# Value blocks placed from PSUM by masked evictions, spread vectors by column strips, and a new order, in a transformer block with sliding attention and a token mixer

## The chip, the cores and the metric

The kernel runs on one core of one Trainium2 chip. The metric is the device time of one execution in microseconds (us); lower is better. The engines are TensorE (PE in the profile, its weight loads PEld), VectorE (DVE), ScalarE (ACT), GpSimd (POOL) and SyncE (SP), whose queue issues almost all DMAs.

## The reference

x is 2048 tokens of 512 features, in bf16. A modulation vector of six parts scales and shifts two branches: sliding-window attention, then a two-layer MLP that mixes along the tokens.

```python
mod = (silu(c) @ w_mod).reshape(1, 6, 1, 512)          # sa, ca, ga, sb, cb, gb
h = layernorm(x) * (1 + ca) + sa
q, k, v = split(h @ wqkv)                              # 32 heads of 16
scores = q @ k.T * 16 ** -0.5, kept where 0 <= i - j < 256
x = x + ga * (softmax(scores) @ v) @ wo
h = layernorm(layernorm(x) * (1 + cb) + sb)
u = gelu(einsum("bsd,sf->bdf", h, w1) + b1)            # over the 2048 tokens, F = 1792
x = x + gb * (einsum("bdf,fs->bds", u, w2) + b2).T
```

## The kernel before

The tokens are cut into four groups of 512 (G = 0 to 3). `proj(G)` normalizes a group, turns it over by DMA (h1T) and multiplies it with wqkv; `attention(G)` runs its scores, exps, masks and sums; `post(G)` multiplies with wo, adds the residual (x) and normalizes twice (h, hb). The first layer of the MLP sums over tokens, so parts of it (pu, part) are done as soon as a group's hb stands, between the chunks of attention; what is left runs after the last group, and then the second layer (py), 238 matmuls in a row, with a store per 128 tokens.

**Keys and values for tiled matmuls.** Scores use rows of 32 and AV sums use column strips of 32, so heads of 16 lie in pairs. Keys (kb, then KT) and values (vb, then VT) are stored twice over, each copy with half of the heads set to zero by a mask per partition (`mask_par`, `mask_half`). A value block `pv` of 128 tokens comes out of PSUM in one cast to `vb` (operation "ve", VectorE or ScalarE); then `place` writes its two halves into VT, `vo` and `vp`, on GpSimd or VectorE. There are four such blocks per group, numbered tb = 0 to 3. Group 0 has its own path, with both halves in one operation.

**Spread vectors.** ga, 1 + cb, sb and gb are needed on all 128 partitions, as rows of 512 (`bc_ga`, `bc_cb1`, `bc_sb`, `bc_gb`). For each, four matmuls with the modulation's silu(c), repeated over 128 columns (`sT_rep`), give the same row on every partition (`ps_b`), and VectorE evicts it. `wod` is wo scaled by bc_ga; the first `post` needs it (`pa`). The others come into `h` (bc_cb1, bc_sb) and into the MLP (bc_gb).

**PSUM.** Scores have five banks (`pss`, three wide, and two of `psb`); all other matmuls share three banks (`ps_od`, tags od0 to od2): projections, AV sums (`po`), wo, the parts and the spread vectors. An operation that takes such a bank waits until what its earlier user put there is evicted.

**Order.** Each operation is an `op` with its possible engines. Two tables set what happens: ORDER, a list of 1,136 numbers, in which the operations are emitted one after the other, and CHOSEN, which takes an operation off its first engine. `run_schedule` emits them so, each engine's instructions keep that order, and every engine and SP's queue run their own list in turn, waiting by semaphores. It also sets `tiled` for runs of projections between AV sums: such a full matmul is then written as four column strips (`mm`), which spares TensorE a change of tiling. All engine calls go through one wrapper, so almost every row of the profile carries its line, L254; rows are told apart by the names of their tiles.

## Time and profile before

| | us |
|---|---|
| runs | 256.61, 259.86, 258.86 (median 258.86) |
| profiled execution | 257.62 |
| its span, first to last instruction | 255.8 |
| busy: TensorE, VectorE, ScalarE, GpSimd | 240.1, 205.5, 172.8, 134.2 |
| last AV sum ends, rest of MLP layer 1 ends | about 178, about 205 |

The span is shorter than the time by 1.8 us of launch and end. A busy time is a union over the span, so it says little of a stage: ScalarE is nearly idle after 181 us, and GpSimd has nothing at all there, while both are close to full between 12 and 120 us.

### The profile page before, as it was taken

How to read it: one execution, taken by the hardware profiler on the slowest of the kernel's cores; microseconds unless marked ns; L12 is line 12 of the kernel's file. 1: busy time of each engine (PE TensorE's matmuls, PEld its weight loads, DVE VectorE, ACT ScalarE, POOL GpSimd, SP SyncE). 2: the span in 40 equal slices, each digit the busy share in tenths (PEclk: the TensorE clock that was granted, in tenths of full speed). 3: DMA queues.
4: the chain of work that ended last, by engine and by line, in shares of the span. 5: the costliest groups of instructions: out<-in, count | busy, mean ns of one | idle time of the engine just before them, and what ended most of it. 6: DMA issues, size and time to landing. Idle time of an engine off the chain costs nothing.

```text
span 255.8 us, 11463 instructions
## 1 busy us (share of the span) xinstructions
PE 240.1 (94%) x5125; PEld 137.7 (54%) x5125; DVE 205.5 (80%) x378; ACT 172.8 (68%) x288; POOL 134.2 (52%) x220
## 2 busy tenths in 40 slices
PE   7999988999889889997999898999999999999995
PEld 3666655656656555655566455557444444444443
DVE  5599998999989979989798879898977974444443
ACT  4699998999998999997899898988207620000000
POOL 6069938967597599969787679964000000000000
PEclk9999999999999999999999999999999999999999
DMA  6998340381032100000621913401699901111111
GB/s 200 327 351 279 68 26 3 82 128 49 3 67 44 27 3 5 4 6 3 177 77 46 249 44 85 122 8 45 179 347 393 352 24 44 41 41 42 60 44 41
DMA packets 39657, 26.44 MB, mean 103 GB/s; under 512 B 11960, under 2 KB 35512, under 8 KB 39608
## 3 DMA queue, kind: packets, MB, share of 16 engines
q1 hardware_dynamic: 39600, 25.71, 35.4%
q8 instruction: 40, 0.66, 1.1%
q14 instruction: 9, 0.07, 0.1%
q10 hardware_dynamic: 8, 0.00, 0.0%
HBM read 22.03 MB, written 2.10 MB: 94 GB/s over the span
## 4 chain that ended last, share of the span: by engine, by line
PE 68%; DVE 16%; ACT 7%; issue 3%; DMA 2%; SPq 2%; POOL 1%; ACTq 0%
PE py L254 19%; PE pu L254 18%; PE po L254 8%; PE pss L254 7%; ACT et L254 7%; DVE et L254 5%; PE pa L254 4%; PE pk L254 3%; PE pq L254 3%; PE pv L254 3%; DVE h L254 2%; DMA x<-in_A_x_dram 2%; DVE st L254 2%; SPq L254 2%; DVE kb L254 2%
## 5 line engine op out<-in xcount | busy, mean ns | idle before, releaser
L254 ACT ACTIVATE et<-pss 128x1536 bf16<-128x1536 f32 (+2 forms) x90 | 101.5, 1147 | 12.0 <-PE psb L254 8.0
L254 PE MATMUL py<-guT,w2r 128*128 128x512 bf16 (+2 forms) x238 | 48.5, 366 | 0.0
L254 ACT ACTIVATE et<-psb 128x512 bf16<-128x512 f32 (+2 forms) x90 | 43.6, 508 | 0.0
L254 DVE TENSOR_TENSOR et<-et,maskt 128x2048 bf16<-128x2048 bf16 (+2 forms) x38 | 42.1, 1120 | 0.4 <-ACT et L254 0.4
L254 PEld LDWEIGHTS <-KT 32*128 32x128 bf16 (+1 forms) x1856 | 24.4, 97 | 30.4 <-issue 26.0
L254 PE MATMUL pu<-hb,w1s 128*32 128x512 bf16 (+1 forms) x260 | 38.8, 380 | 0.8 <-DVE part L254 0.7
L254 PE MATMUL pss<-QT,KT 32*64 32x32 bf16 (+7 forms) x1392 | 34.8, 202 | 4.8 <-ACT et L254 2.2
L254 PE MATMUL po<-et,VT 128*32 128x256 bf16 (+2 forms) x960 | 33.4, 234 | 3.8 <-DVE vb L254 2.2
L254 PEld LDWEIGHTS <-w2r 128*128 128x128 bf16 x238 | 22.8, 98 | 25.9
L254 PE MATMUL psb<-QT,KT 32*128 32x224 bf16 (+3 forms) x464 | 34.3, 203 | 0.9 <-issue 0.9
L254 PE MATMUL po<-et,ones_bd 128*32 128x256 bf16 (+3 forms) x624 | 31.4, 269 | 0.5 <-issue 0.5
L254 DVE TENSOR_TENSOR otile<-py,xr 128x512 bf16<-128x512 f32 (+2 forms) x17 | 11.2, 660 | 24.6 <-PE py L254 24.5
L254 POOL TENSOR_SCALAR KT<-kb,mask_par 128x512 bf16<-128x512 bf16 (+1 forms) x30 | 21.1, 714 | 13.2 <-DVE kb L254 11.8
L254 PEld LDWEIGHTS <-VT 128*32 128x32 bf16 x960 | 21.7, 96 | 10.8 <-issue 3.8
L254 DVE BATCH_NORM_STATS2 st<-x 128x6 f32<-128x512 bf16 x32 | 21.3, 680 | 2.0 <-DMA x<-in_A_x_dram 1.9
L254 POOL TENSOR_SCALAR VT<-vb,mask_half 128x512 bf16<-128x512 bf16 x25 | 20.1, 810 | 4.9 <-DVE vb L254 4.4
L254 PEld LDWEIGHTS <-w1s 128*32 128x32 bf16 (+1 forms) x260 | 13.9, 97 | 14.5 <-issue 1.2
L254 PE MATMUL pk<-h1T,wqkv 128*32 128x512 bf16 (+4 forms) x222 | 20.7, 333 | 0.0
L254 PEld LDWEIGHTS <-wqkv 128*32 128x32 bf16 (+1 forms) x380 | 15.2, 96 | 8.8 <-issue 1.1
L254 PE MATMUL pu<-hb,w1r 128*128 128x512 bf16 (+1 forms) x84 | 18.0, 380 | 0.0
L254 PE MATMUL pv<-wqkv,h1T 128*32 128x256 bf16 x512 | 17.6, 274 | 0.1
L254 PE MATMUL pa<-wod,OT 128*32 128x512 bf16 (+1 forms) x130 | 16.7, 381 | 0.2 <-DVE x L254 0.2
(107 smaller groups left out, 365.3 us busy)
## 6 DMA issues: line engine op xcount, KB each, us to landing
w2r<-in_B_w_dram SPq DMA_DIRECT2D x14, 512.0 KB, 10.5
w1s<-in_B_w_dram SPq DMA_DIRECT2D x19, 256.0 KB, 3.3
w1r<-in_B_w_dram SPq DMA_DIRECT2D x9, 256.0 KB, 4.9
x<-in_A_x_dram SPq DMA_DIRECT2D x16, 128.0 KB, 4.9
wmod<-in_w_mod_dram SPq DMA_DIRECT2D x4, 512.0 KB, 8.5
out_dram<-otile SPq DMA_DIRECT2D x15, 128.0 KB, 1.7
wmod<-in_w_mod_dram SPq DMA_DIRECT2D x4, 256.0 KB, 3.4
wqkv<-in_A_wqkv_dram SPq DMA_DIRECT2D x4, 256.0 KB, 5.2
```

What stands on the lines that cost most here:

```text
L254: ins = call(*args, **kwargs)
```

## The change

1. For the blocks tb = 2 and 3 of groups 1 to 3 (DIRECT_V), the cast to vb is dropped. Two masked operations, "vd", read the block in PSUM and write the two halves of VT. They may run on VectorE or ScalarE; the bank is free after both.
2. ScalarE is allowed as an engine for the normalizations, the copies of et ("xc") and the placements of K and V.
3. The matmuls for the four spread vectors run in strips of 32 columns side by side, into one bank; `sT_rep` shrinks to 32 columns. One eviction (`bcs`) applies a factor and an addend per partition (`bc_fix`), and four DMAs on SP's queue spread each strip over 128 partitions.
4. ORDER and CHOSEN are new throughout (1,125 operations). In the built program all twelve "vd" stand on VectorE, and ScalarE takes one et copy and no placement. Counts by engine that differ: VectorE 380 to 373 instructions, of them `vb` casts 14 to 8, `KT<-kb` 8 to 4 (six of 512 columns gone, two of 256 more), et copies 15 to 8, evictions of spread vectors 4 to 1, `h`, `hb` and `xn` normalizations four more, casts of Q two fewer. GpSimd: `VT<-vb` 25 to 14, `KT<-kb` of 512 columns 18 to 24 and of 256 12 to 10, et copies 13 to 19, `hb` 11 to 9, `h` and `xn` one fewer each. ScalarE: one more `kb` of 256 columns and one fewer of 512, one more QT of 256 and one of 512, one et copy more. TensorE: the same work as before but for the spread vectors, though more of it is written in strips (5,125 to 5,239 matmuls); scores are entered 75 times in both.

Where the spread vectors are evicted on VectorE, in group 0's attention (`x_..` are statistics for later groups, `et` the exps, `OT` the finished sums). Before:

```order
L254 CAST bc_sb<-ps_b 128x512
L254 BN_STATS st<-x_80 128x6
L254 BN_STATS st<-x_77 128x6
L254 TENSOR_TENSOR OT_0_136<-po,lz 128x256
L254 BN_STATS st<-x_74 128x6
L254 TENSOR_SCALAR bc_ga<-ps_b 128x512
L254 COPY et<-et 128x16x32
L254 TENSOR_TENSOR OT_1_137<-po,lz 128x256
L254 CAST vb<-pv 128x512
L254 TENSOR_TENSOR et<-et,maskt 128x16x2x64
L254 TENSOR_SCALAR VT_167<-vb,mask_half 128x32x16 x2
L254 TENSOR_SCALAR bc_cb_118<-ps_b 128x512
```

And now:

```order
L255 TENSOR_SCALAR bcs<-ps_b,bc_fix 128x512
L255 CAST vb<-pv 128x512
L255 TENSOR_TENSOR et<-et,maskt 128x4x128
L255 TENSOR_TENSOR et<-et,maskt 128x4x64
L255 TENSOR_SCALAR VT_167<-vb,mask_half 128x32x16 x2
L255 TENSOR_TENSOR OT_0_136<-po,lz 128x256
L255 BN_STATS st<-x_75 128x6
L255 TENSOR_TENSOR OT_1_137<-po,lz 128x256
L255 BN_STATS st<-x_76 128x6
L255 TENSOR_TENSOR OT_2_138<-po,lz 128x256
L255 BN_STATS st<-x_73 128x6
L255 BN_STATS st<-x_74 128x6
```

Four evictions (bc_gb stood a little earlier) have become one. Behind these rows come a full mask, OT_3, four multiplies of h1T, one cast of kb, and then the first two multiplies of wod by bc_ga.

SP's queue at the same place, before:

```order
L254 DMA x_79<-in_A_x_dram 128x512
L254 DMA x_80<-in_A_x_dram 128x512
L254 DMA_TRANSPOSE h1T_181<-xn 128x4x128 x4
L254 DMA b1b<-in_B_b_dram 128x14x1
L254 DMA b2b<-in_B_b_dram 128x16x1
L254 DMA w1s_1856<-in_B_w_dram 128x4x256
L254 DMA_TRANSPOSE h1T_180<-xn 128x4x128 x4
L254 DMA w1s_2189<-in_B_w_dram 128x4x256
```

And now:

```order
L255 DMA x_79<-in_A_x_dram 128x512
L255 DMA x_80<-in_A_x_dram 128x512
L255 DMA_TRANSPOSE h1T_181<-xn 128x4x128 x4
L255 DMA bc_ga<-bcs 128x1x512
L255 DMA b1b<-in_B_b_dram 128x14x1
L255 DMA b2b<-in_B_b_dram 128x16x1
L255 DMA bc_gb<-bcs 128x1x512
L255 DMA bc_cb_118<-bcs 128x1x512
L255 DMA_TRANSPOSE h1T_180<-xn 128x4x128 x4
L255 DMA bc_sb<-bcs 128x1x512
L255 DMA w1s_2165<-in_B_w_dram 128x4x256
L255 DMA_TRANSPOSE h1T_181<-xn 128x4x128 x3
```

bc_ga stands behind the turning of group 1's xn (h1T_181), bc_gb and bc_cb ahead of that of group 2 (h1T_180), and the first w1s behind it.

VectorE late in the third group's projection (VT_169), before:

```order
L254 CAST vb<-pv 128x512
L254 CAST QT_2_149<-pq 128x512
L254 BN_STATS st<-h_2578 128x6
L254 BN_STATS st<-h_2530 128x6
L254 TENSOR_TENSOR et<-et,maskt 128x16x2x64
L254 CAST kb<-pk 128x512
L254 TENSOR_TENSOR OT_2_142<-po,lz 128x256
L254 TENSOR_SCALAR VT_169<-vb,mask_half 128x32x16
L254 COPY et<-et 128x16x32
L254 TENSOR_TENSOR OT_3_143<-po,lz 128x256
L254 TENSOR_TENSOR et<-et,maskt 128x16x2x64
L254 TENSOR_SCALAR VT_169<-vb,mask_half 128x32x16
```

And now:

```order
L255 COPY et<-et 128x16x32
L255 CAST kb<-pk 128x512
L255 TENSOR_TENSOR et<-et,maskt 128x16x2x64
L255 TENSOR_SCALAR VT_169<-pv,mask_half 128x32x16
L255 TENSOR_TENSOR et<-et,maskt 128x16x2x64
L255 TENSOR_SCALAR VT_169<-pv,mask_half 128x32x16
L255 TENSOR_TENSOR OT_3_143<-po,lz 128x256
L255 TENSOR_SCALAR VT_169<-vb,mask_half 128x32x16
L255 CAST kb<-pk 128x512
L255 TENSOR_TENSOR OT_2_142<-po,lz 128x256
```

Before, a block left PSUM in one cast, `vb<-pv`; now the two halves `VT<-pv` stand apart, with a whole mask between them.

```diff
--- before.py
+++ after.py
@@ -59,77 +59,78 @@
 LATENCY = {"PE": 0.18, "ACT": 0.15, "DVE": 0.13, "POOL": 0.15, "SP": 2.0}
 COLUMN = 1 / 2400.0
 E_BUFS = 3
+DIRECT_V = [(1, 2), (1, 3), (2, 2), (2, 3), (3, 2), (3, 3)]
+DIRECT_K = []
 E_COLS = 1280
...
@@ -501,7 +502,13 @@
     rm = modw.tile([ND, P], F32, name="rm")
     silu4 = modw.tile([ND, P], BF, name="silu4")
     sT = modw.tile([P, ND], BF, name="sT")
-    sT_rep = modw.tile([P, ND, P], BF, name="sT_rep")
+    sT_rep = modw.tile([P, ND, 32], BF, name="sT_rep")
+    bcs = modw.tile([P, D], BF, name="bcs")
+    bc_fix = modw.tile([P, 2], F32, name="bc_fix")
+    nc.gpsimd.memset(bc_fix[:, 0:1], 1.0)
+    nc.gpsimd.memset(bc_fix[0:32, 0:1], ZSCALE)
+    nc.gpsimd.memset(bc_fix[:, 1:2], 0.0)
+    nc.gpsimd.memset(bc_fix[32:64, 1:2], 1.0)
     def e_warm(e, n):
         if "warm" not in box:
             box["warm"] = ps_a.tile([P, 3, D], F32, name="pss")
@@ -530,8 +537,8 @@
     o5 = op("st", "PE", 0.1, e_stps, deps=[o4], pos=-20, cls="D", alloc="od")
     o6 = op("sT", "DVE", 0.15, lambda e: ve.tensor_copy(out=sT[:], in_=box["st"][:]), deps=[o5], pos=-20)
     o5.frees = [o6]
-    o_rep = op("sTrep", "DVE", 0.35, lambda e: ve.tensor_copy(
-        out=sT_rep[:], in_=sT[:].unsqueeze(2).to_broadcast([P, ND, P])), deps=[o6], pos=-6, ready=15.0)
+    o_rep = op("sTrep", "DVE", 0.2, lambda e: ve.tensor_copy(
+        out=sT_rep[:], in_=sT[:].unsqueeze(2).to_broadcast([P, ND, 32])), deps=[o6], pos=-6, ready=15.0)
 
     def e_fm(k):
         if k == 0:
@@ -566,30 +573,31 @@
         return first, o
 
     mod_ops = []
-    for n, (v, dst) in enumerate(((2, bc_ga), (4, bc_cb1), (3, bc_sb), (5, bc_gb))):
-        def e_bc(n, v=v):
-            if n == 0:
-                box["bc", v] = bank([P, D], F32, "ps_b")
-            for k in (2 * n, 2 * n + 1):
+    vectors = ((2, bc_ga), (4, bc_cb1), (3, bc_sb), (5, bc_gb))
+
+    def e_bc(n):
+        if n == 0:
+            box["bc"] = bank([P, D], F32, "ps_b")
+        for k in (2 * n, 2 * n + 1):
+            for i, (v, _) in enumerate(vectors):
                 te.matmul(
-                    box["bc", v][:], lhsT=sT_rep[:, k, :], rhs=wmod[:, k, v * D : (v + 1) * D],
-                    start=(k == 0), stop=(k == ND - 1),
+                    box["bc"][32 * i : 32 * i + 32, :], lhsT=sT_rep[:, k, :], rhs=wmod[:, k, v * D : (v + 1) * D],
+                    start=(k == 0), stop=(k == ND - 1), tile_position=(0, 32 * i), skip_group_check=True,
                 )
 
-        def e_bce(e, v=v, dst=dst):
-            if v == 2:
-                ve.tensor_scalar(
-                    out=dst[:], in0=box["bc", v][:], scalar1=ZSCALE, scalar2=0.0, op0=ALU.mult, op1=ALU.add,
-                )
-            elif v == 4:
-                ve.tensor_scalar_add(out=dst[:], in0=box["bc", v][:], scalar1=1.0)
-            else:
-                ve.tensor_copy(out=dst[:], in_=box["bc", v][:])
-
-        a, z = dense(f"bc{v}", [0.435] * 2, e_bc, [o_rep], 9.0 + n, cls="D", alloc="od", ready=22.0)
-        b = op(f"bce{v}", "DVE", 0.6, e_bce, deps=[z], pos=9.0 + n)
-        a.frees = [b]
-        mod_ops.append(b)
+    def e_bce(e):
+        ve.tensor_scalar(
+            out=bcs[:], in0=box["bc"][:], scalar1=bc_fix[:, 0:1], scalar2=bc_fix[:, 1:2], op0=ALU.mult, op1=ALU.add,
+        )
+
+    bc_first, bc_last = dense("bc", [0.435] * 2, e_bc, [o_rep], 9.0, alloc="od", ready=22.0)
+    bce = op("bce", "DVE", 0.6, e_bce, deps=[bc_last], pos=9.0)
+    bc_first.frees = [bce]
+    for n, (v, dst) in enumerate(vectors):
+        def e_bb(e, n=n, dst=dst):
+            dma.dma_start(out=dst[:], in_=bcs[32 * n : 32 * n + 32, :].unsqueeze(1).to_broadcast([32, ND, D]))
+
+        mod_ops.append(op("bb", "SP", 0.65, e_bb, deps=[bce], pos=9.0 + n, extra=1.0))
 
     def e_b12(e):
         ve.tensor_copy(out=b1FM[:], in_=b1b[:])
@@ -645,6 +653,8 @@
             ENGINE[e].tensor_scalar(
                 out=dst, in0=src, scalar1=mv[:, i, 0:1], scalar2=rs[:, i : i + 1], op0=ALU.subtract, op1=ALU.mult,
             )
+        elif e == "ACT":
+            ac.activation(out=dst, in_=src, func=ACT.Identity, scale=rs[:, i : i + 1], bias=nm[:, i : i + 1])
         else:
             ENGINE[e].tensor_scalar(
                 out=dst, in0=src, scalar1=rs[:, i : i + 1], scalar2=nm[:, i : i + 1], op0=ALU.mult, op1=ALU.add,
@@ -686,11 +696,16 @@
                     start=(dc == 0), stop=(dc == ND - 1), tile_position=(0, QB * r), skip_group_check=True,
                 )
 
-    def place(eng, dst, src, tb, half):
-        eng.tensor_scalar(
-            out=dst[:, 2 * tb : 2 * tb + 2, :, half * DH : (half + 1) * DH],
-            in0=src[:].rearrange("p i (a d) -> p i a d", d=DH),
-            scalar1=mask_half[:, half : half + 1], scalar2=0.0, op0=ALU.mult, op1=ALU.add,
+    def masked(e, out, in_, mask):
+        if e == "ACT":
+            ac.activation(out=out, in_=in_, func=ACT.Copy, scale=mask)
+        else:
+            ENGINE[e].tensor_scalar(out=out, in0=in_, scalar1=mask, scalar2=0.0, op0=ALU.mult, op1=ALU.add)
+
+    def place(e, dst, src, tb, half):
+        masked(
+            e, dst[:, 2 * tb : 2 * tb + 2, :, half * DH : (half + 1) * DH], src[:].rearrange("p i (a d) -> p i a d", d=DH),
+            mask_half[:, half : half + 1],
         )
 
     def proj0():
...
@@ -1000,22 +1015,30 @@
                     box["v", tb] = bank([P, 2, 256], F32, "pv")
                 values(box["v", tb], h1T, tb, n)
 
-            def e_ve(e):
+            def e_ve(e, vb_tag):
                 box["vb", tb] = work.tile([P, 2, 256], BF, name="vb", tag=vb_tag, bufs=1)
                 copy(e, box["vb", tb][:], box["v", tb][:])
 
-            vb_tag = turn("vb", 3)
             war = [av_ops[G - 2, g] for g in range(ND)] if G >= 2 else []
             a, z = dense("v", [0.431] * 2, e_v, h_ops, pos, alloc="od", ready=11.5)
             mms.append(z)
-            ve_op = op("ve", {"ACT": 0.5, "DVE": 0.6}, 0.6, e_ve, deps=[z], pos=pos)
-            a.frees = [ve_op]
-            placed = [
-                op(("vo", "vp")[half], {"POOL": 0.78, "DVE": 0.45}, 0.78,
-                   lambda e, half=half: place(ENGINE[e], VT[r3], box["vb", tb], tb, half), deps=[ve_op] + war, pos=pos)
-                for half in range(2)
-            ]
-            slot(vb_tag, ve_op, *placed)
+            if (G, tb) in DIRECT_V:
+                placed = [
+                    op("vd", {"ACT": 0.5, "DVE": 0.61}, 0.5,
+                       lambda e, half=half: place(e, VT[r3], box["v", tb], tb, half), deps=[z] + war, pos=pos)
+                    for half in range(2)
+                ]
+                a.frees = placed
+            else:
+                vb_tag = turn("vb", 3)
+                ve_op = op("ve", {"ACT": 0.5, "DVE": 0.6}, 0.6, lambda e: e_ve(e, vb_tag), deps=[z], pos=pos)
+                a.frees = [ve_op]
+                placed = [
+                    op(("vo", "vp")[half], {"POOL": 0.78, "DVE": 0.45, "ACT": 0.5}, 0.78,
+                       lambda e, half=half: place(e, VT[r3], box["vb", tb], tb, half), deps=[ve_op] + war, pos=pos)
+                    for half in range(2)
+                ]
+                slot(vb_tag, ve_op, *placed)
             v_done[G, tb] = placed
 
         for n, pos in sorted(p_at.items(), key=lambda f: f[1]):
@@ -1261,9 +1284,12 @@
                 for unit in units:
                     def e_xc(e, k=unit["tile"]):
                         src, dst = runs_of(et_of[k], 0, QB + HQ, RUN, 4), runs_of(et_of[k], 0, 0, QB, 4)
-                        ENGINE[e].tensor_copy(out=dst, in_=src)
-
-                    unit["copied"] = op("xc", {"DVE": 0.27, "POOL": 0.6}, 0.27, e_xc, deps=[ea, eb], pos=i + M_POS)
+                        if e == "ACT":
+                            ac.activation(out=dst, in_=src, func=ACT.Copy)
+                        else:
+                            ENGINE[e].tensor_copy(out=dst, in_=src)
+
+                    unit["copied"] = op("xc", {"DVE": 0.27, "POOL": 0.6, "ACT": 0.5}, 0.27, e_xc, deps=[ea, eb], pos=i + M_POS)
             for unit in ends:
                 def e_mu(e, k=unit["tile"]):
                     dst = et_of[k][:].rearrange("p j (r n s) -> p (j r) n s", n=5, s=KB)[:, :, 0:5:4, :]
```

61 lines of the change are left out of this document (30 added, 31 removed), and 119 rows, old and new, of tables (CHOSEN, ORDER).

## Prediction

> **What bounds the kernel now.** I read the page first, then a table of stages, then the waits of TensorE and of ScalarE. The page says that no engine is far behind the others, and that TensorE carries the chain:
>
> ```profile
> PE 240.1 (94%) x5125; PEld 137.7 (54%) x5125; DVE 205.5 (80%) x378; ACT 172.8 (68%) x288; POOL 134.2 (52%) x220
> PE 68%; DVE 16%; ACT 7%; issue 3%; DMA 2%; SPq 2%; POOL 1%; ACTq 0%
> ```
>
> Shares over the span mislead here, because the last 75 us are TensorE alone. So I cut the span at the ends of the stages (start, first half-group of attention, two middle stretches, the end of attention, the rest of MLP layer 1, layer 2):
>
> ```profile
> 12.00:40.00 28.00, 25.85 (x767) 17.73 (x766) 27.77 (x65) 27.45 (x49) 20.05 (x38) 1.00 0.68 175
> 40.00:80.00 40.00, 36.82 (x1159) 23.63 (x1154) 37.44 (x66) 37.65 (x60) 31.97 (x49) 1.00 0.31 57
> 80.00:120.00 40.00, 35.95 (x1222) 23.13 (x1222) 36.48 (x57) 37.22 (x62) 33.01 (x46) 1.00 0.05 10
> 120.00:181.00 61.00, 59.16 (x1563) 34.31 (x1548) 53.61 (x91) 51.62 (x87) 44.87 (x60) 1.00 0.33 92
> 181.00:205.00 24.00, 24.00 (x113) 10.88 (x111) 20.21 (x46) 11.41 (x20) 0.00 (x0) 1.00 0.95 332
> 205.00:255.80 50.80, 48.19 (x238) 22.48 (x235) 23.73 (x38) 1.42 (x3) 0.00 (x0) 1.00 0.13 42
> ```
>
> The columns are PE, PEld, DVE, ACT, POOL, granted clock (1.00 throughout), DMA share, GB/s. From 12 to 40 us VectorE is the fullest (27.77 of 28) with ScalarE beside it (27.45). From 40 to 120 us three engines are at 90 to 94 per cent: a loop in which each waits a little for each other one. From 120 us on TensorE takes over, and after 181 us it never stops. Which waits are left between 12 and 181 us:
>
> ```profile
> PE po L254 <- DVE vb L254: 2.2, 3, 1.3
> PE pss L254 <- ACT et L254: 2.2, 5, 0.7
> ACT et L254 <- PE psb L254: 8.0, 18, 1.2
> ACT et L254 <- PE pss L254: 3.4, 7, 1.1
> DVE OT L254 <- ACT lz L254: 3.7, 7, 0.9
> ```
>
> ScalarE waits 11.4 us for scores, so it is not a hard bound, though it has little else to give. TensorE's longest such wait, 1.3 us, is for the copy of a value block, and the timeline shows why it was late:
>
> ```profile
> 116.91 2.18 DVE L254 TENSOR_TENSOR et<-et,maskt 128x2048 bf16<-128x2048 bf16 x1
> 118.08 2.02 POOL L254 TENSOR_TENSOR h<-h,bc_sb 128x512 bf16<-128x512 bf16 x1
> 119.00 0.68 DVE L254 CAST vb<-pv 128x512 bf16<-128x512 f32 x1
> 119.74 0.41 PE L254 MATMUL po<-et,VT 128*32 128x256 bf16 x12 [1.31 <-DVE vb L254]
> ```
>
> A mask multiply of 2.18 us stood ahead of the copy, while GpSimd worked beside it. So VectorE's queue is what lets TensorE down, and the work on it decides more than its share says.
>
> **The change, part 1: the spread vectors.** Four vectors of the modulation were spread over 128 partitions by 16 full matmuls of 512 columns, and evicted four times. Now the 16 run in column strips of 32, four side by side; one eviction takes all four strips, and four DMAs spread them further.
>
> ```profile
> L254 PE MATMUL py<-guT,w2r 128*128 128x512 bf16 x210 | 45.5, 379 | 0.0
> L254 PE MATMUL ps_b<-wmod,sT_rep 128*128 128x512 bf16 x16 | 4.3, 382 | 0.0
> L254 PE MATMUL pu<-hb,w1s 128*32 128x512 bf16 x144 | 9.7, 380 | 0.0
> L254 DVE TENSOR_SCALAR bc_ga<-ps_b 128x512 bf16<-128x512 f32 x1 | 0.7, 667 | 0.0
> ```
>
> In a steady run a full matmul takes 45.5 / 210 = 0.217 us of TensorE. The strips of pu show what four side by side take: 9.7 / 36 quads = 0.27 us, as much as one of the 16 full ones (4.3 / 16 = 0.27). So 16 become 4 slots: at the steady rate 12 x 0.217 = 2.6 us less, by the busy rows 12 x 0.27 = 3.2 us. I take 2.6. VectorE loses three of four evictions, 3 x 0.67 = 2.0 us, in the stretch in which it is the fullest.
>
> What is added are four transfers on SP's queue. The trace has no copy from SBUF to SBUF of this kind; small transfers near it are these:
>
> ```profile
> h1T<-xn SPq DMA_TRANSPOSE x12, 3.0
> b2b<-in_B_b_dram SPq DMA_DIRECT2D x1, 4.0 KB, 5.8
> out_dram<-otile SPq DMA_DIRECT2D x1, 32.0 KB, 1.4
> L254 DVE TENSOR_TENSOR wod<-wod,bc_ga x4: 401/408/542, 37.9 to 48.3; 128x512 bf16<-128x512 bf16 x4
> L254 DVE BATCH_NORM_STATS2 st<-x 128x6 f32<-128x512 bf16 x32 | 21.3, 680 | 2.0 <-DMA x<-in_A_x_dram 1.9
> L254 DVE TENSOR_TENSOR OT<-po,lz 128x256 bf16<-128x256 f32 x32 | 13.3, 415 | 3.8 <-ACT lz L254 3.7
> ```
>
> So 1.4 to 5.8 us each, I take 3. The first one that anybody waits for is bc_ga, by the scaling of wod on VectorE. In the new order 19 instructions of VectorE stand between the eviction and that scaling (the first place shown with the change): four statistics (2.7 us), four OT multiplies (1.7), two casts of a block (some 1.1), four h1T and two VT at about 0.4 each (2.4), a full mask and two short ones (some 2.1). That is 10 us. Ahead of bc_ga on SP stand the four transposes whose h1T comes just before wod, so those are waited for in any case. The transfer is covered by these 10 us, with 4 to spare at 5.8. Without this cover VectorE would stand 3 to 5.8 us, and with it the scores of the next group. bc_cb, bc_sb and bc_gb are needed tens of microseconds later; what queues behind them on SP (transposes of the third group, then the first w1s) is due later too. Price of the DMAs: nothing, at worst 5.8.
>
> **Part 2: six value blocks placed straight from PSUM.** Before, a block was cast to SBUF once and then placed in two masked halves, mostly by GpSimd:
>
> ```profile
> L254 DVE CAST vb<-pv 128x512 bf16<-128x512 f32 x14 | 9.5, 680 | 0.5 <-PE pv L254 0.5
> L254 POOL TENSOR_SCALAR VT<-vb,mask_half 128x512 bf16<-128x512 bf16 x25 | 20.1, 810 | 4.9 <-DVE vb L254 4.4 <-ACT vb L254 0.5
> L254 DVE TENSOR_SCALAR VT<-vb,mask_half 128x512 bf16<-128x512 bf16 x7 | 2.8, 406 | 0.0
> L254 DVE TENSOR_SCALAR VT<-vb,mask_half x7: 341/342/780, 32.8 to 136.1; 128x512 bf16<-128x512 bf16 x7
> ```
>
> Now six casts go (6 x 0.68 = 4.1 us of VectorE) and 12 masked halves read PSUM. The order shows all twelve on VectorE. The trace has no such form; the nearest row is bc_ga, a TENSOR_SCALAR of the same size from PSUM at 0.667, and casts of it take 0.680. 12 x 0.68 = 8.2 us. The bound below is 0.34 us (the fastest VT<-vb from SBUF, 341 ns), which I exclude since the casts and bc_ga, which read 512 f32 columns of PSUM as these do, stand at 0.67 to 0.68. So VectorE gains 4.1 us of work from this part, and GpSimd loses 11 placements, 11 x 0.81 = 8.9 us.
>
> [...]
>
> A bank of PSUM is now held over two evictions, 0.68 us longer per block. There are three banks for projections and AV sums together. Against this, AV no longer waits for a second hop. Both ends lie within about 2.2 us (all that TensorE waits for vb now, in 3 cases); I take zero.
>
> **Part 3: what moved with the new order.** The counts by engine and form of the two orders, priced by these rows:
>
> ```profile
> L254 POOL TENSOR_SCALAR KT<-kb,mask_par 128x512 bf16<-128x512 bf16 x18 | 15.4, 866 | 4.5 <-DVE kb L254 3.2 <-ACT kb L254 1.3
> L254 DVE TENSOR_SCALAR KT<-kb,mask_par 128x512 bf16<-128x512 bf16 x6 | 2.3, 420 | 0.0
> L254 POOL COPY et<-et 128x512 bf16<-128x512 bf16 x13 | 9.3, 717 | 9.6 <-ACT et L254 9.6
> L254 DVE COPY et<-et 128x512 bf16<-128x512 bf16 x15 | 4.7, 323 | 1.2 <-ACT et L254 1.2
> L254 POOL TENSOR_SCALAR hb<-h,rs,nm 128x512 bf16<-128x512 bf16 x11 | 11.8, 1077 | 0.3
> L254 ACT ACTIVATE QT<-pk 128x256 bf16<-128x256 f32 x2 | 0.8, 418 | 0.2 <-DVE kb L254 0.2
> L254 ACT ACTIVATE part<-pu 128x512 f32<-128x512 f32 x2 | 1.2, 588 | 3.1 <-PE pu L254 3.1
> ```
>
> VectorE: six placements of KT go to GpSimd (-6 x 0.42 = -2.5), seven copies of et go (-7 x 0.32 = -2.3), two smaller casts of Q go to ScalarE (-1.1); four normalizations come from GpSimd (+1.8), and a few of 0.3 to 0.4 each cancel. With parts 1 and 2 VectorE's sum is -4.1 + 8.2 - 2.0 - 2.5 - 2.3 - 1.1 + 1.8 = -2.0 us. But two multiplies of the last normalization move from behind the last OT to ahead of it (+1.1), so up to the end of attention it is -0.9.
>
> GpSimd: +6 KT (5.2), +6 et (4.3), -11 VT (8.9), -2 hb (2.2), about -2.8 of others: -4.4 us. ScalarE: one kb and two QT more (0.4 to 0.6 each), one kb less, one copy of et (no row; between 0.42 and 0.59): +1.4 us, and an eviction of part moved to ahead of the last scores, +0.6: +2.0 us. It is the only engine that gets more. TensorE: 38 more full matmuls are written as quads of strips; a quad costs what one full matmul does (0.27 each above), so only part 1 counts, and blocks of scores are entered as often as before.
>
> **The sum.** In the stages up to 120 us each engine must give way for time to be saved, from 120 us only TensorE. TensorE -2.6. The wait for vb and the longer hold of banks: 0 (bounds -2.2 and +4.1, six holds of 0.68). VectorE's -0.9 to -2.0: no gain of its own beside TensorE's, since both are in the loop. ScalarE's +2.0 is covered by its 11.4 us of waiting for scores; where the loop has no slack it costs, and I charge a sixth, +0.3. GpSimd's -4.4 lets VectorE's masks run nearer their fast form: GpSimd's share falls by 3 per cent, priced at nothing. Sum -2.3. Against the profiled execution, 257.62 us (span 255.8 and 1.8 around it), that gives **255.3 us**. The median of the three runs shown is 258.86, 1.2 above the profiled one, so part of what will be read as gain would be that difference; 2% of the median is 5.2 us, about what a measurement of this kernel can tell from no change.
>
> **The rivals.** (a) VectorE's queue is the real bound up to 120 us, and its relief pays more than TensorE's. For it: 27.77 of 28 us, and the wait at 119.74. Summing VectorE's rows ahead of each of the 28 full masks in both orders at the prices above, the new order has 2 to 5 us less ahead of the tenth to the twenty-fifth mask, mostly 4; if that comes through beside 1.7 us of TensorE after 120 us: 257.6 - 5.7 = 251.9 us. Against: the work comes back before the end of attention, and TensorE's own work has to fit.
>
> [...]
>
> ```profile
> L254 DVE TENSOR_TENSOR et<-et,maskt 128x2048 bf16<-128x2048 bf16 x28 | 38.7, 1383 | 0.4 <-ACT et L254 0.4
> L254 DVE TENSOR_TENSOR et<-et,maskt x38: 279/1212/2179, 17.7 to 175.3; 128x2048 bf16<-128x2048 bf16 x28, 128x512 bf16<-128x512 bf16 x6, 128x256 bf16<-128x256 bf16 x4
> ```
>
> If each of 28 masks gained 0.17 us (1.38 against 1.21, the median of all masks), that would be 4.8 us on VectorE, the same size.
>
> (b) ScalarE is the bound and the gain does not appear: the spread vectors are saved where TensorE would have waited for exps anyway. For it: 37.65 and 37.22 of 40. Then -2.6 is lost in waiting and +1.4 to +2.0 comes on top: 257.6 + 1.4 = 259 us. Against: its 11.4 us of waiting for scores.
>
> (c) The slower side: banks are held too long. In the third projection the order puts a whole mask between the two halves of a directly placed block, so its bank is held 0.68 + 1.38 + 0.68 = 2.7 us, up to 3.5 if the mask runs at 2.18. Six blocks by 0.68, plus this mask, plus the OT multiply (0.42) between another's halves: 4.1 + 1.4 to 2.2 + 0.4 = 5.9 to 6.7 us of bank time. It decides once the other two banks are full, held by an AV sum and a projection, when the next projection starts; passed to TensorE in full it is 257.6 - 2.6 + 6.7 = 261.7 us. Against: most of it overlaps other work, and a whole wait for vb costs 2.2 now.
>
> **How the numbers follow.** Forecast 0.52, (a) 0.23, (b) 0.16, (c) 0.09. The forecast's own range is 252.8 to 257. The range of 8 in 10 takes in (a) below, with 1.4 us more, and (b) above: 250.5 to 259.5. Faster by over 2%, under 253.7: nearly all of (a), 0.20, and 0.09 from the forecast's lower edge: 0.29. Slower by over 2%, over 264.0: a third of (c) and a little of (b): 0.04. Within: 0.67.
>
> **What would show it.** Right: ps_b at about 1.1 us in all instead of 4.3; VT<-pv on VectorE at 0.68 (x12); POOL near 130 us, DVE near 203.5; no wait of wod for a DMA; TensorE between 12 and 181 us still short of full, with the last stage from the end of attention on at 24 + 51 us. Rival (a) shows as DVE short of full from 12 to 40 and hardly any wait of po for VectorE; (b) as ACT et waiting less than 9 us for scores; (c) as waits of pk, pq or po for VT on VectorE of over 3 us. The forecast is wrong if the granted clock falls below 1.00, if wod waits for bc_ga, or if masks get slower than 1.38 us in the mean.

## The result, and the profile after

The change made the kernel slower by about one per cent: 260.07 us (258.25 to 262.38, 20 executions) against 257.45 us for the kernel before on the same chip. The ratio is 1.0094, with a 95% interval of 1.0070 to 1.0119. The prediction said 255.3 us. The profiled execution took 259.75 us, with a span of 258.1.

The page of the changed kernel, its engines and the row of the granted clock:

```profile
PE 239.2 (93%) x5239; PEld 138.0 (53%) x5239; DVE 207.2 (80%) x371; ACT 175.0 (68%) x291; POOL 129.9 (50%) x219
PEclk9998899999999999999999999999999999999999
```

TensorE's busy time is hardly lower (240.1 before) although 2.6 us of it were taken out, VectorE's has risen by 1.7 us instead of falling by 2.0, and the clock has a dent in the fourth and fifth slice. The stages, and two-microsecond pieces of the first one (columns as in the prediction):

```profile
12.00:40.00 28.00, 22.02 (x752) 16.26 (x744) 24.78 (x60) 24.47 (x41) 18.12 (x35) 0.94 0.74 181
40.00:80.00 40.00, 36.52 (x1184) 23.59 (x1176) 37.46 (x59) 36.97 (x62) 33.60 (x49) 1.00 0.33 65
80.00:120.00 40.00, 37.25 (x1166) 23.12 (x1159) 36.70 (x57) 38.21 (x63) 37.54 (x51) 1.00 0.10 25
120.00:181.00 61.00, 59.32 (x1718) 35.57 (x1716) 57.09 (x91) 57.09 (x95) 35.97 (x53) 1.00 0.34 92
...
20.00:22.00 2.00, 0.66 (x24) 0.37 (x14) 2.00 (x4) 1.62 (x2) 2.00 (x4) 1.00 1.09 346
22.00:24.00 2.00, 1.26 (x46) 1.03 (x50) 0.71 (x4) 0.50 (x1) 1.59 (x7) 1.00 0.99 311
24.00:26.00 2.00, 2.00 (x32) 0.82 (x24) 0.69 (x3) 1.82 (x5) 0.94 (x3) 0.52 0.40 105
26.00:28.00 2.00, 2.00 (x56) 0.93 (x52) 2.00 (x7) 0.72 (x3) 2.00 (x3) 0.62 0.03 9
```

The loss shows in the first row: TensorE, VectorE and ScalarE each do 3 to 4 us less there than before, and the clock is 0.94. At 20 us TensorE stops while the DMA engines run full (share 1.09, 346 GB/s), and from 24 to 28 us it runs at about half clock (0.52 and 0.62). TensorE's timeline shows the stop, and its waits have it as one piece:

```profile
20.05 0.60 PE L255 MATMUL pv<-wqkv,h1T 128*32 128x256 bf16 x14
...
22.73 0.72 PE L255 MATMUL pv<-wqkv,h1T 128*32 128x256 bf16 x18 [2.08 <-issue]
...
25.13 1.90 PE L255 MATMUL ps_b<-wmod,sT_rep 128*32 128x512 bf16 x16
```

```profile
PE pss L255 <- ACT et L255: 5.6, 13, 1.1
...
PE pv L255 <- issue: 2.1, 1, 2.1
```

The stop falls in the middle of one value block, between its 14th and 15th matmul, and waits for nothing that the profile shows ("issue"). What the trace has near it is a fetch of instructions. The page's DMA part counts those (packets, MB, share), so 16 KB each:

```profile
q8 instruction: 41, 0.67, 1.1%
```

The 41 fetches here stand against 10,478 weight loads and matmuls, the 40 of the kernel before against 10,250. By division that is one fetch to some 256 of them in both; which engine a fetch is for, the rows do not say.

The records of the trace tie the stop to a fetch. Ahead of it they have 354 records of the weight loads' queue (351 of them weight loads) and 351 matmuls, and the three versions below that stop as well (a_light, b_quads, f_quads) stop at the same count, to one record, although b_quads keeps the old order. The second fetch of the run starts at 20.1 us, and the 355th record of that queue goes at 22.7, 2.6 us later. In none of the 20 traces of this case is that distance under 2.4 us. The kernel before, whose second fetch starts at 21.4 us, comes to its 355th record only at 24.2, 2.8 us later, and does not stop. In the new order nearly all key and query projections of the first group are quads (full matmuls written as four column strips): 192 matmuls of 32 columns where the kernel before had 48. So TensorE has its 354 records behind it earlier, at 20.3 us instead of 24.1, in the middle of the bulk loads. That it has run out of fetched instructions there is the author's reading; no row shows what it waits for.

The groups on which the prediction's prices rested:

```profile
L255 DVE TENSOR_SCALAR VT<-pv,mask_half 128x512 bf16<-128x512 f32 x12 | 8.6, 740 | 0.4 <-PE pv L255 0.4
L255 DVE TENSOR_TENSOR et<-et,maskt 128x2048 bf16<-128x2048 bf16 x28 | 37.5, 1343 | 0.2
L255 DVE TENSOR_SCALAR hb<-h,rs,nm 128x512 bf16<-128x512 bf16 x3 | 2.0, 657 | 0.0
L255 DVE TENSOR_SCALAR VT<-vb,mask_half 128x512 bf16<-128x512 bf16 x6 | 3.3, 561 | 0.0
L255 PE MATMUL ps_b<-wmod,sT_rep 128*32 128x512 bf16 x16 | 1.9, 628 | 0.0
```

The direct placements cost 0.74 us each instead of 0.68. The normalizations that VectorE took over cost 0.66 instead of the 0.45 that was charged. The strips took 1.9 us instead of 1.1, because they ran at half clock (a_whole below has the same 16 in 1.05 us, at full clock).

### The profile page after: what moved, and what is told of

Same layout as the page of the kernel before. It is cut to its first block, busy times and chain, and to the rows that moved or that the text cites. A ratio compares the mean times of both kernels' runs of the same rounds, so it can differ in the third digit from the quotient of the medians.

```text
span 258.1 us, 11707 instructions
## 1 busy us (share of the span) xinstructions
PE 239.2 (93%) x5239; PEld 138.0 (53%) x5239; DVE 207.2 (80%) x371; ACT 175.0 (68%) x291; POOL 129.9 (50%) x219
## 5 line engine op out<-in xcount | busy, mean ns | idle before, releaser
L255 PEld LDWEIGHTS <-KT 32*128 32x128 bf16 (+1 forms) x1856 | 25.1, 97 | 29.7 <-issue 25.4
L255 PE MATMUL po<-et,VT 128*32 128x256 bf16 (+2 forms) x960 | 32.8, 234 | 2.5 <-DVE part L255 0.8
L255 POOL TENSOR_SCALAR KT<-kb,mask_par 128x512 bf16<-128x512 bf16 (+1 forms) x34 | 25.8, 770 | 12.2 <-DVE kb L255 11.6
L255 PE MATMUL po<-et,ones_bd 128*32 128x256 bf16 (+3 forms) x624 | 30.6, 269 | 0.0
L255 PEld LDWEIGHTS <-VT 128*32 128x32 bf16 x960 | 20.9, 96 | 10.2 <-issue 2.4
L255 DVE BATCH_NORM_STATS2 st<-x 128x6 f32<-128x512 bf16 x32 | 21.4, 682 | 2.0 <-DMA x<-in_A_x_dram 1.8
L255 PE MATMUL pk<-h1T,wqkv 128*32 128x256 bf16 (+4 forms) x312 | 21.6, 312 | 0.0
L255 POOL COPY et<-et 128x512 bf16<-128x512 bf16 x19 | 12.6, 669 | 8.3 <-ACT et L255 8.3
```

Source lines behind the costliest of these rows:

```text
L255: ins = call(*args, **kwargs)
```

## The experiments

Every version was compared with the kernel before on the same chip; "ratio" is to that kernel. The summary first. The third column counts the executions whose mean granted clock was under 0.996; of 131 executions of the kernel before on the chips of these sets it was 27.

| version | median us | clock low | ratio (95%) |
|---|---|---|---|
| the change | 260.07 | 13 of 20 | 1.0094 (1.0070 to 1.0119) |
| a_whole | 258.64 | 6 of 10 | 1.0076 (1.0044 to 1.0108) |
| b_quads | 261.28 | 4 of 6 | 1.0171 (1.0133 to 1.0209) |
| b_whole | 255.72 | 2 of 12 | 0.9934 (0.9906 to 0.9962) |
| a_light | 257.49 | 6 of 12 | 1.0016 (0.9989 to 1.0042) |
| a_noquad | 258.46 | 6 of 12 | 1.0061 (1.0030 to 1.0092) |
| b_noquad | 257.65 | 1 of 12 | 0.9998 (0.9967 to 1.0029) |
| a_fill | 258.28 | 2 of 12 | 1.0010 (0.9974 to 1.0045) |
| f_quads | 261.37 | 6 of 6 | 1.0181 (1.0137 to 1.0224) |
| a_putback | 258.04 | 2 of 12 | 1.0069 (1.0037 to 1.0101) |
| f_putback | 260.04 | 0 of 6 | 1.0128 (1.0080 to 1.0175) |
| b_strips | 256.42 | 7 of 12 | 0.9990 (0.9960 to 1.0020) |
| a_vbdve | 258.41 | 6 of 12 | 1.0058 (1.0027 to 1.0090) |
| b_direct | 258.99 | 0 of 12 | 1.0070 (1.0044 to 1.0096) |
| a_vdhalf | 259.25 | 10 of 12 | 1.0062 (1.0027 to 1.0097) |
| a_vbpool | 263.59 | 6 of 6 | 1.0199 (1.0162 to 1.0236) |
| f_maskcut | 256.06 | 1 of 12 | 0.9974 (0.9944 to 1.0003) |
| f_poolcut | 257.11 | 1 of 12 | 1.0007 (0.9979 to 1.0035) |

**The early quads.** a_whole is the changed kernel with the first group's key and query projections as whole matmuls (48 quads fewer, 12 of which the kernel before has too); b_whole is the same edit in the kernel before; b_quads makes them all quads there (56 instead of 12).

```diff
-                    mm(box["kq", g8][:, n, :], wqkv[:, dc, w0 : w0 + P], h1T[:, dc, cols], (dc == 0), (dc == ND - 1))
+                    te.matmul(box["kq", g8][:, n, :], lhsT=wqkv[:, dc, w0 : w0 + P], rhs=h1T[:, dc, cols], ...)
```

For b_quads, instead, `Op.quad = True` ahead of the `mm`.

> The changed kernel, with the key and query projections of the first group written as 36 fewer quads, that is as whole matmuls of 128 columns in place of four strips each. The work on the data is the same; TensorE has some 288 fewer instructions (weight loads and matmuls) to take in, nearly all before 25 us. Theory (early strips: TensorE runs out of fetched instructions while the bulk loads fill the DMA queues, stands 2.1 us for nothing that the profile shows, and the granted clock then falls): the pause of 2.08 us before pv is gone or under 0.5, the granted clock of 12 to 40 us is back at 1.00, ps_b takes about 0.27 a matmul instead of 0.63, and the time is 255 to 256.5 us, 4 to 5 below the change and 1 to 2 below the kernel before. Rival (the early loss comes from the new order, for example from the wait for kb or for the modulation's weights): the time stays within 1 us of the change's 260.

> The kernel before, with one edit: the key and query projections of the first group are all written in quads of strips, as most of them are in the change (264 more instructions of TensorE). Nothing else of the change is in it: old order, old spread vectors, no value block straight from PSUM. Theory (early strips): 3 to 5 us slower than the kernel before, with a pause of about 2 us near 20 us that waits for nothing shown, and a granted clock under 1.00 in the slices behind it. Rival (the new order or the new waits make the loss): within 0.7 us of the kernel before, no such pause.

> The kernel before, with the key and query projections of the first group all written whole (72 fewer instructions of TensorE; 12 quads of 36 matmuls were strips there). If fetched instructions already ran short a little before the change (pauses named issue of 0.7 to 0.9 us in its waits), it is 0.3 to 1 us faster than the kernel before; if the loss starts only where the fetch falls behind the bulk loads, it is the same within 0.4 us.

In the old order the expectation held. b_quads is 1.7% slower, 4.4 us, with nothing else changed, and the same stop is there:

```profile
22.66 1.36 PE L254 MATMUL pk<-h1T,wqkv 128*32 128x256 bf16 x30 [2.53 <-issue]
```

b_whole is 0.66% faster than the kernel before, so even its 12 early quads cost 1.7 us, more than was expected and without a stop in the profile; how they do it is not shown. It is the fastest of all versions, and beats both kernels. In the changed kernel the stop went too, and the profiled execution of a_whole ran at full clock throughout. But its median fell by little: the ratio went from 1.0094 to 1.0076, which the intervals don't tell apart. That is the rival's outcome for the time and the theory's for the stop. Six of its ten executions still had a low clock, so something else pulled it down.

**The bulk loads.** a_light leaves out three of the four loads of the modulation's weights for the spread vectors and uses the first for all strips.

```diff
-    for v in (2, 4, 3, 5):
+    for v in (2,):
```

> The changed kernel with three of the four loads of the modulation's weights for the spread vectors left out (1.5 MB less; all four strips use the first, so three of the four vectors are not what they should be; TensorE's work is the same). The bulk loads end some 4 us earlier. If the pause of TensorE at 20 us is an instruction fetch that comes late because the queues are full, the pause shrinks below 1 us or goes, and the time is 255.5 to 257.5. If the fetch is simply asked for too late, whatever the load on the queues, or the pause has another cause, it stays at about 2 us and the time at 259.5 to 260.5.

The time came out where the first case had it, 0.8% under the change. The pause halved, but did not go:

```profile
21.38 0.72 PE L255 MATMUL pv<-wqkv,h1T 128*32 128x256 bf16 x18 [1.12 <-issue]
```

The second fetch starts at 19.0 us here instead of 20.1. So about half of the stop (2.08 to 1.12 us) went with the three loads, and the other half stays when the DMA engines move only 76 GB/s at that time instead of 346 (window 20 to 22 us). The pause was 1.1 us, just above the bound that was set. But the time fell by 2.0 us, more than the pause did, and below a_whole, which has no stop around 20 us; what else the lighter loads gave is not shown.

**Quads elsewhere.** a_noquad and b_noquad write every matmul of the helper whole (`if True:` in place of `if not Op.quad:` in `mm`).

> The changed kernel with all projections and other matmuls of the helper written whole, none as quads of strips (about a thousand fewer instructions of TensorE); a change of tiling between them and the sums then falls on TensorE again. If TensorE's stream of instructions costs time in the whole program and not only near 20 us, this is faster than the whole-matmul version of the first projection alone, by 1 us or more. If the strips pay outside the start, it is 0.5 to 3 us slower than that version.

> The kernel before with every matmul of the helper written whole, none in strips (about 800 fewer instructions of TensorE than before). With all of them whole the changed kernel took the same time as with the first projection alone whole; so this is within 0.7 us of the kernel before with its first projection whole, that is 0.7 to 2.4 us under the kernel before. Rival: the strips pay in the old order, where TensorE has fewer pauses to hide a change of tiling in: 1 us or more above that version.

In the changed kernel the rest of the quads neither pay nor cost (1.0061 against 1.0076). In the old order they do pay: b_noquad is 0.64% behind b_whole, the rival's case. So it is not quads that are bad, but quads early in the program: 44 more of them cost 4.4 us in b_quads.

**The clock.** A second run of a_whole was to give another profile (a_whole2).

> The whole-matmul version of the change once more, for a profile of another execution: seven of its ten earlier executions had a mean granted clock of 0.986 to 0.998 and took 1 to 3 us longer than the three at 1.00. If the clock falls after a pause of TensorE, a profile with a mean under 1.00 shows slices of 0.5 to 0.6 right behind a pause of 1 us or more between 26 and 36 us, where the mean busy share of TensorE in the first profile is lowest. Rival: the low slices stand elsewhere, with no such pause ahead.

It took 257.93 us, again at full clock, and decided nothing. But the profile of a_noquad caught a low stretch, and so did those of a_vdhalf and a_vbpool (versions of a_whole, below), all between 32 and 40 us; a_vbpool has a second one at 79 us, behind a wait of 1.7 us. In the windows of a_noquad, 26 to 34 and 34 to 38 us:

```profile
26.00:34.00 8.00, 4.81 (x224) 3.78 (x216) 7.68 (x15) 7.97 (x17) 6.51 (x12) 1.00 0.41 71
34.00:38.00 4.00, 3.92 (x84) 2.73 (x83) 3.20 (x9) 2.76 (x4) 3.67 (x9) 0.60 0.73 36
```

TensorE is busy for 4.81 of 8 us, then the clock is 0.60 in the mean of 4 us (half clock for 3.4 us). There is no long stop ahead of it, only short ones, none over 0.8 us. The same window, 26 to 34 us, in a_whole and in b_whole:

```profile
26.00:34.00 8.00, 4.88 (x217) 3.85 (x217) 7.84 (x16) 7.97 (x17) 6.63 (x12) 1.00 0.43 72
```

```profile
26.00:34.00 8.00, 7.54 (x279) 4.99 (x270) 8.00 (x17) 8.00 (x16) 6.65 (x11) 1.00 0.40 65
```

The new order leaves TensorE 61% busy there, the old one 94%, while ScalarE is full in both. a_fill puts idle matmuls into these pauses, on a_whole:

```diff
                     unit["ps"] = bank([P, 2, HQ], F32, "po")
+                    for _ in range(2 if unit["G"] == 0 else 0):
+                        te.matmul(unit["ps"][:], lhsT=nothing[:, 0:P], rhs=nothing[:], start=True, stop=True, ...)
```

> The whole-matmul version of the change, with two idle matmuls of 512 columns (zeros) ahead of each group of sums in the first quarter of attention, where TensorE's pauses are: some 16 x 0.217 = 3.5 us more of TensorE, before sums that wait for exps. Theory (the granted clock falls when TensorE is busy only 55 to 70 per cent over some 8 us, as the profile with all matmuls whole shows between 26 and 34 us ahead of its low slices at 34 to 38): the mean clock over the executions rises from 0.994 to 0.998 or more, and the median falls by 0.3 to 1.2 us in spite of the added work. Rival (the clock has another cause, or the added matmuls stand on the path): clock as before, 0.5 to 3.5 us slower.

The low clock came in 2 of 12 executions instead of 6 of 10, and the ratio fell by 0.66% although TensorE had 3.5 us more to do (the two intervals just touch). TensorE in that window, now:

```profile
26.00:34.00 8.00, 6.63 (x232) 4.07 (x224) 7.85 (x15) 7.52 (x17) 6.46 (x9) 1.00 0.57 71
```

This is the second cause: work taken out of TensorE where it waits anyway can cost clock. The profiles of all versions bear it out. The 20 traces have eight falls of the clock between 22 and 180 us, and ahead of each, TensorE's matmuls cover 72% of the last 8 us or less, ahead of five of them 66% or less. Eight versions, the kernel before among them, have no 8 us under 74% in that stretch of their traces; none of these traces has a fall, and 34 of their 209 executions had a low clock. Of the other versions' executions it was 72 of 120. It is not a sure sign: a_putback (below) goes down to 60% and had the low clock in 2 of 12. Among the 20 executions of the change, the median of the seven at full clock is 258.92 us, so by this split the low clock is worth 1.15 us of the 260.07. TensorE did not have to be idle for a whole stretch (a_noquad: 4.81 of 8 us busy, no wait over 0.8 us).

With the pauses filled the quads' price stands out. f_quads is the change with its early quads and the same filling.

> The change as it is, early quads included, with the sixteen idle matmuls ahead of the sums in the first quarter of attention. The pause of 2.1 us at 20 us comes ahead of them and stays. If most of the quads' cost is that pause and the low clock right behind it, this is 1.5 to 3 us slower than the filled version with whole matmuls, and the profile shows the low slices at 24 to 28 us again. If the cost came from the later drops of the clock alone, it is within 0.7 us of it.

It is 1.7% behind a_fill, 4.4 us, as in the old order, and more than was expected. The stop is 2.65 us long here, the profile has half clock right behind it (0.50 from 24 to 26 us), and all six executions had a low clock. So the 4.4 us are the stop and the clock together.

**What the spread vectors are worth.** a_putback adds to a_whole what the strips saved, 12 full matmuls and three evictions; f_putback does it on a_fill; b_strips brings the strips alone into the old order, on b_whole.

```diff
             box["bc"] = bank([P, D], F32, "ps_b")
+            for i in range(12):
+                te.matmul(box["bc"][:], lhsT=warm[:, 0:P], rhs=warm[:], start=True, stop=True, ...)
...
+        for i in range(3):
+            ve.tensor_copy(out=bcd[:], in_=box["bc"][:])
```

> The whole-matmul version of the change (first run of this set), with the old price of the spread vectors put back: 12 more full matmuls of 512 columns ahead of the strips and three more evictions on VectorE, whose results nobody uses. The prediction's term for the spread vectors, 2.6 us on the path: this run is 2.0 to 2.8 us slower than the first one. Rival (TensorE would have waited there anyway for exps or for VectorE): less than 1 us slower.

> The filled version with whole matmuls, plus the old price of the spread vectors: 12 more matmuls of 512 columns ahead of the strips and three more evictions on VectorE. The prediction's term: 2.0 to 2.8 us slower than the filled version. Rival (the loop of attention waits for another engine and takes most of it back; without the filling the put-back version was 0.9 us behind at the end of attention and no slower over all executions): 0 to 1 us slower.

> The kernel before in its old order, first projection whole, with one part of the change: the four spread vectors in strips side by side in one bank (12 matmul slots of 0.22 to 0.27 us less), one eviction in place of four, four DMAs on SP's queue (the first behind three of the four transposes of the second group, the others behind the fourth). The prediction's term: 2.0 to 2.6 us faster than the same kernel without this part, that is a ratio of about 0.984 to 0.986 to the kernel before. Rival (TensorE would have waited there for exps or VectorE anyway): a ratio of 0.991 or more. A second rival: the DMAs come late and wod or the transposed second group wait for them, which shows as a wait and a ratio over 0.995.

Putting the price back cost nothing in the new order as it is (1.0069 against 1.0076): the added matmuls only filled pauses, and the low clock came in 2 of 12. With the pauses filled already it cost 1.2%, 3.0 us by the ratios (1.0 us by the two profiled spans, 257.6 against 256.6). So the prediction's 2.6 us is about the right size of the work, and the new order has room for it that is otherwise lost in waiting. b_strips shows the same in the old order, where it was expected to pay most. It is 0.56% slower than b_whole. Window 24 to 40 us, b_whole first, then b_strips:

```profile
24.00:40.00 16.00, 13.57 (x467) 9.11 (x472) 15.05 (x32) 15.56 (x28) 12.05 (x17) 1.00 0.41 53
```

```profile
24.00:40.00 16.00, 10.85 (x449) 8.30 (x449) 14.01 (x27) 15.03 (x27) 12.40 (x17) 0.96 0.65 86
```

TensorE lost 2.7 us of work, VectorE 1.0, and ScalarE did no more than before. TensorE's wait for the exps, b_whole first, then b_strips:

```profile
PE pss L254 <- ACT et L254: 1.5, 5, 0.7
```

```profile
PE pss L254 <- ACT et L254: 4.5, 8, 1.3
```

The 2.7 us taken out came back as 3.0 us of waiting for ScalarE. And the clock fell from 38 us on (0.59 in 38 to 42 us); 7 of 12 executions had a low clock. No wait in the profile names one of the four DMAs, so the second rival is out.

**What the direct value blocks are worth.** b_direct puts the two masked placements from PSUM where the cast stood, in the old order, on b_whole. The other three start from a_whole. a_vbdve undoes the direct placements: one cast, two placements from the copy, all on VectorE. a_vbpool is the same with `place("POOL", ...)`, so GpSimd has both placements again; the copies of both go through one buffer, which the profile calls `nothing`. a_vdhalf cuts the second half to an eighth.

```diff
-                op("vd", ..., lambda e, half=half: place(e, VT[r3], box["v", tb], tb, half), ...)
...
+                    if ("vb", tb) not in box or box["vb", tb] != G:
+                        box["vb", tb] = G
+                        copy(e, vb[:], box["v", tb][:])
+                    place(e, VT[r3], vb, tb, half)
```

> The whole-matmul version of the change, with the direct placements undone: each of the six value blocks is cast from PSUM to SBUF once, and both masked halves are then written from that copy, all on VectorE at the places where the direct ones stood. VectorE's work by the prediction's rows: 0.68 + 2 x 0.34 to 0.41 = 1.36 to 1.5 us a block against 2 x 0.74 as measured direct, so equal; but the bank of PSUM is free after the cast, 0.68 us earlier, and before the mask that stands between the halves. The prediction charged the longer hold of banks at nothing: then this run is within 0.6 us of the whole-matmul version. Rival (c) of the prediction (banks held too long): 1.5 to 6 us faster than it.

> The kernel before in its old order, first projection whole, with one part of the change: the six value blocks placed straight from PSUM by two masked operations on VectorE each, where the cast stood; GpSimd is rid of their placements. VectorE gets 6 x (2 x 0.74 - 0.68) = 4.8 us less the two placements it did itself (0.8), GpSimd loses about 8 us. The prediction called this part a draw: then the ratio to the kernel before stays at 0.990 to 0.997, within 0.4 per cent of the version without it. Rival (VectorE's work counts in the old order): 1.5 to 4 us slower, a ratio of 1.000 to 1.009. Rival (GpSimd's relief counts, since the placements are waited for): a ratio under 0.988.

> The whole-matmul version of the change, with the six direct value blocks given back to the old way in full: one cast on VectorE, both masked halves on GpSimd at the same places of the order. VectorE loses 12 x 0.74 - 6 x 0.68 = 4.8 us, GpSimd gets 12 x 0.83 = 10 us, and the blocks go through one SBUF buffer, so a cast can wait for the placements before it. If VectorE's work sets the pace: 1.5 to 4 us faster than the whole-matmul version. If GpSimd has no room left where the new order already gave it the placements of K: the same or slower, with sums waiting for VT on GpSimd.

> The whole-matmul version of the change, with the second masked half of each of the six direct value blocks cut to an eighth of its columns (the rest of that half of V is left out; it is set to zero once, before the work starts). VectorE is rid of about 6 x 0.65 = 3.9 us, half of it before the first third of attention ends; nothing goes to another engine, and the banks are free 0.65 us earlier each. Theory (VectorE's work sets the pace in attention, and the change put more on it than the prediction reckoned): 2 to 4 us faster than the whole-matmul version. Rival (ScalarE or TensorE sets the pace): less than 0.8 us faster.

Among themselves the two ways on VectorE are equal (a_vbdve 1.0058, a_whole 1.0076), and an earlier free bank brings nothing: rival (c) is out for the new order. But moving the placements from GpSimd to VectorE is no draw. In the old order it costs 1.36%, 3.5 us, though GpSimd loses 11 us. TensorE now waits for VectorE's placements (b_direct):

```profile
PE po L254 <- DVE VT L254: 1.9, 2, 1.4
PE po L254 <- DVE vb L254: 1.7, 2, 1.3
...
PE pu L254 <- DVE VT L254: 0.6, 1, 0.6
```

In b_whole it waits for the casts of the blocks:

```profile
PE po L254 <- DVE vb L254: 2.4, 3, 1.3
```

In the new order the way back is closed too. GpSimd has been given the placements of K, and a_vbpool is 1.2% slower than a_whole (all six of its executions had a low clock, so part of this is the clock); its placements take 1.04 us each:

```profile
L255 POOL TENSOR_SCALAR VT<-nothing,mask_half 128x512 bf16<-128x512 bf16 x12 | 12.4, 1039 | 2.7 <-DVE nothing L255 2.7
```

a_vdhalf brought no gain, but 10 of its 12 executions had the low clock, so it settles nothing about VectorE by itself.

**Who sets the pace.** Two cuts on a_fill, where the clock holds: half of each full mask of the first two groups left out (f_maskcut: `rows = 8 if unit["G"] <= 1 else 16`), and GpSimd's multiplies and adds by the spread vectors cut to 64 of 512 columns (f_poolcut).

> The filled version with whole matmuls, with half of each full mask multiply of the first two groups left out (11 or 12 masks, about 0.65 us each: 7 to 8 us of VectorE less before half of attention is done; nothing goes to another engine). If VectorE sets the pace of the new order: 2.5 to 6 us faster than the filled version. If it does not (cutting 3.9 us of its work brought nothing without the filling): less than 1 us faster.

> The filled version with whole matmuls, with seven eighths of GpSimd's ten multiplies and adds by the spread vectors left out (five of each, 1.2 to 1.3 us: some 10.5 us of GpSimd less, most of it between 55 and 120 us, where the new order has it at 37.5 of 40 us against 33 before). If GpSimd sets the pace there, with the placements of K, V and the copies of et queued behind these multiplies: 2 to 5 us faster than the filled version. If it is only busy and not waited for: less than 1 us faster.

Neither engine is the bound alone. Twelve masks went from about 1.35 to 0.79 us, 6.7 us less for VectorE, and the ratio fell by 0.36%, 0.9 us, which the intervals don't tell from nothing. GpSimd's ten operations went from about 12.5 us to 5.3, less than planned, and brought nothing that can be told. What is left full and untried is ScalarE, with 7.97 of 8 us from 26 to 34 us in a_whole (VectorE has 7.84). It was not relieved by itself in any run, so that it sets the pace there is read from the windows and the waits, and not shown by an experiment.

## Why the prediction was wrong, by its own steps

- **The quads (the step that failed first).** "38 more full matmuls are written as quads of strips; a quad costs what one full matmul does": this holds for the time of TensorE's array in the prediction's rows (0.27 us for either), and leaves out its instructions. A quad is four weight loads and four matmuls instead of one each, and the term was put at nothing. In the old order 44 more early quads alone cost 4.4 us (b_quads); with the pauses filled, the 48 of the change cost as much (f_quads). In the change as it stands taking them out gives only 0.2%. Against the profile of a_whole the seventh exp of pss starts 4.0 us later and the 88th 2.5 us later, so part of the delay is made up; that a_whole's own falls of the clock hide the rest is likely, and not shown. The order of TensorE showed these rows; only the array's time was priced.
- **Part 1, -2.6 us.** The work was sized about right, its place was wrong. From 12 to 40 us ScalarE had 27.45 of 28 us in the prediction's own first row, and what is taken out of TensorE there comes back as waiting for exps (b_strips: 0.56% slower instead of 1% faster). Rival (b) said this ("saved where TensorE would have waited for exps anyway") and its sign, ScalarE waiting less than 9 us for scores, came true: 6.2 + 1.3 us against 11.4 before. Its 259 us lie near the measured time partly by luck, since it priced neither the stop nor the clock. Rival (a)'s sign came too (VectorE has 24.78 of 28 us from 12 to 40, and TensorE's longest wait of po for VectorE is 0.8 us), and yet the time rose: VectorE was short of work behind the stop of TensorE (0.71 of 2 us from 22 to 24), and not relieved. The forecast charged TensorE's saving in full because it looked at the whole span up to 120 us.
- **Part 2, which the sum has at zero** (the expectation of b_direct calls it a draw). 12 x 0.74 - 6 x 0.68 is +4.8 us, 0.7 more than reckoned, and the relief of GpSimd was worth less than VectorE's load: 3.5 us slower alone (b_direct). The bank's longer hold, priced at nothing, was right in the new order (a_vbdve).
- **Part 3.** VectorE was to fall by 2.0 us and rose by 1.7. The normalizations (hb) and the placements from SBUF took longer, 0.66 and 0.56 us (rows above) against 0.45 and 0.41; that GpSimd's work beside them is the reason is likely, and not shown. (Of the full masks in the same profile, the six that ran while GpSimd was idle took 1.21 to 1.22 us, those with GpSimd busy beside them 1.21 to 2.13.) GpSimd's 129.9 us and the four DMAs, covered by other work (three with 2.6 to 5.3 us to landing, wod waiting for none), came as forecast. The masks stayed at 1.34 us.
- **The granted clock.** The text named a clock under 1.00 as what would make it wrong, but gave it no price. It is 1.15 us of the median by the split above.

Added up from b_whole (0.9934): the strips alone +0.56%, the direct blocks alone +1.36%, together 1.0126 if they simply add, which was not tried. The change without its early quads is at 1.0076, so by this sum the new order gives back about half a per cent; with them it is at 1.0094. What the order gives back was not tried apart from the rest.

## What to carry to other kernels

Ask of every microsecond taken out of an engine what that engine waits for in that stage: where another engine is full, the saving becomes a pause (b_strips: 2.7 us out, 3.0 us of waiting), and on TensorE many short pauses went with a low clock here (6 of 10 executions of a_whole, 2 of 12 with the pauses filled). When all engines are near full, relief of one brought little here (0.36% in f_maskcut, 0.03% in f_poolcut) and load on one cost nearly in full (b_direct, 3.5 us for 4.8), so an edit that moves work from one to another needs a stage-by-stage account and not totals. And count instructions as well as array time: column strips multiply them by four, which cost nothing in mid-kernel in the new order (1.0076 with them, 1.0061 without) and 4.4 us early, in the middle of the bulk loads (b_quads).

## What the runs showed of the hardware that was not expected

- TensorE stood 2.1 to 2.7 us around 20 us with no wait that the profile shows, with the DMA engines at 346 to 348 GB/s (the change, b_quads, f_quads), and 1.1 us at 76 GB/s, with three of the four DMAs for the weights of the spread vectors left out (a_light). All four stops came behind the 354th record of the weight loads' queue, and the 355th went 2.4 to 2.7 us behind the start of a fetch.
- The clock does not need a long stop to fall: 8 us with TensorE 62 to 69% busy, and but for the second fall of a_vbpool no pause over 1.3 us, were followed by half clock, mostly for 3.4 us, in some executions (a_noquad, a_vdhalf, a_vbpool, b_strips), and by none in others (a_whole, a_light).
- Sixteen idle matmuls, 3.5 us of work, went with a ratio 0.66% lower (a_fill against a_whole).
